# A new head: q and k further ahead, k's squares added on GpSimd, the column norms computed beside the last scores, and x and mean squares of two blocks interleaved

## The chip, the cores and the metric

The kernel runs on one core of one Trainium2 chip. The metric is device time in microseconds: the median of the timed runs of the whole program. One profiled execution of the kernel gives the trace that every row below comes from.

## What is computed

The reference is a channel attention followed by two feed-forward stages, all on 6016 tokens with 256 channels, in float32:

```python
qn = q / (norm(q, axis=1) + 1e-6)           # norm over the 6016 tokens, one per channel
kn = k / (norm(k, axis=1) + 1e-6)
s = kn.transpose(0, 2, 1) @ qn / tau        # 256 x 256
a = softmax(s)
x = v @ a                                   # 6016 x 256
xn = x / sqrt(mean(x*x, -1) + 1e-6) * rms_g
y = (silu(xn @ w_gate) * (xn @ w_val)) @ w_out      # inner width 1536
h = y @ w_in                                # inner width 2048
out = (h - tanh(h)) @ w_out2
```

## The kernel before

All large products after the head are made as three TensorE passes (`mm3`, L82 to L84): each operand is split into a high part (`hi_of`, ScalarE, L75) and a low part (`lo_of`, VectorE, L78). Weights arrive as pairs of 32-bit words and are converted by a generator, `conversion()`: for each block of 512 columns `wNraw` it runs a copy on ScalarE (L136, result `wNy`), a shift on VectorE (L183), two VectorE combinations (L189, L195), the split on ScalarE (L75, `wNh`) and the subtraction on VectorE (L78, `wNl`). One pump of the generator does one of four steps; `PLAN` says how many pumps run at each labelled place of the program, and `at(...)` runs them. A block that a product needs and that isn't converted yet is converted on the spot. Raw weights have three buffers, so a later weight load waits for a conversion; the order of loads is that of the program on SP's one queue. `("s", i)` labels the place after chunk `i` of the head, `("c", n)` places between the last scores and the first gate product, `("g", ...)` and `("h", ...)` places in the two feed-forward stages.

The order on each engine is that of the program text: the schedule is manual, and every engine works through its own list.

The head is `attention()`. q and k come in chunks of token rows; per chunk ScalarE squares q and k (L325; the first ones straight into `acc`, L321), VectorE adds them into `acc` (L326), and TensorE adds k-transposed times q into two accumulators `S0` and `S1` (L308, two products for each of the 47 rows of a chunk; the profile has two records for each float32 product, so 188 records, 16 for a chunk of 4 rows). The squares of the two are of one size and go through two `sq` buffers. The last two chunks' scores wait until `nrm` (L345), a product of `acc` with a column of ones, has given TensorE the sums of squares. VectorE then takes the inverse root (L354 to L362, 15 small operations), spreads q's factors over the partitions (`dq`, L366, then the product `rq_ps`, L370) and forms the softmax of the two halves (L381 to L392). The result `a` feeds `x` (L412), which is v times a for the first two blocks of 512 tokens.

The head is followed, block by block, by `x_post`: squares on ScalarE (L437), mean squares `ms` on TensorE (L479, eight narrow products per block), the inverse root on VectorE (L485 to L96), its spread over partitions (`d`, L491, product `r`, L497), `xg` (x times the gain, ScalarE L443, times `r`, VectorE L505), and the split of that into `x0h` and `x0l` for block 0, `x1h` and `x1l` for block 1. Blocks 0 and 1 are then multiplied by the gate and value weights, feature by feature: `g` and `v` (L82 to L84), silu on ScalarE (L545) and the product on VectorE (L546, `t`). Block 1's post-work is spread over the first features of block 0's products (`POST`).

Before the change the first four chunks are loaded ahead and chunk `i+4` after chunk `i`'s scores:

```python
r = sp.tile([P, W, C], F32, tag=f"raw{nm}", bufs=4, name=f"{nm}{i}")
...
load(i + 4)
if i in W_LOADS:
    j = W_LOADS.index(i)
    w_load(w_queue[j], *((sp, EARLY_RAW) if j < EARLY_RAW else ()))
```

Of the kernel before, what the change touches and what calls it, by code (L numbers as in the profile page):

```python
# [794 lines left out]
```

## Time and profile before

| what | value |
|---|---|
| median of 3 timed runs | 1209.13 us (1208.88 to 1210.33) |
| the profiled execution | 1206.14 us, of which 1204.3 us are its span |
| TensorE busy in the span | 1186.8 us (99%) |
| VectorE, ScalarE, GpSimd busy | 681.1, 536.2 and 0.7 us |
| mean granted TensorE clock | 0.995 |

The profiled execution lies 2.99 us below the median of the timed runs. A time below that is "in the span" counts from the first instruction of the execution. An idle time in a row is that of the row's engine just before the instruction, with the work that ended it. "PEclk" is the granted TensorE clock as a share of full speed, 1.00 for 2.4 GHz and 0.50 for 1.2 GHz.

### The profile page before, as it was taken

How to read it: one execution, taken by the hardware profiler on the slowest of the kernel's cores; microseconds unless marked ns; L12 is line 12 of the kernel's file. 1: busy time of each engine (PE TensorE's matmuls, PEld its weight loads, DVE VectorE, ACT ScalarE, POOL GpSimd, SP SyncE). 2: the span in 40 equal slices, each digit the busy share in tenths (PEclk: the TensorE clock that was granted, in tenths of full speed). 3: DMA queues.
4: the chain of work that ended last, by engine and by line, in shares of the span. 5: the costliest groups of instructions: out<-in, count | busy, mean ns of one | idle time of the engine just before them, and what ended most of it. 6: DMA issues, size and time to landing. Idle time of an engine off the chain costs nothing.

```text
span 1204.3 us, 13571 instructions
## 1 busy us (share of the span) xinstructions
PE 1186.8 (99%) x5310; PEld 988.9 (82%) x5310; DVE 681.1 (57%) x1119; ACT 536.2 (45%) x930; POOL 0.7 (0%) x6
## 2 busy tenths in 40 slices
PE   8889999999999999999999999999999999999998
PEld 6668888888888888888888888888888888888998
DVE  5888779653384384375356347347337437436534
ACT  6556556543343354254344344344335325425434
POOL 0000000000000000000000000000000000000000
PEclk9999999999999999999999999999999999999999
DMA  9534332001001000000000000100100000000000
GB/s 340 208 107 123 89 104 88 18 19 35 1 1 36 1 1 20 16 1 18 18 1 18 18 1 1 35 1 1 35 1 1 32 1 1 18 1 1 18 1 14
DMA packets 20640, 43.33 MB, mean 36 GB/s; under 512 B 1889, under 2 KB 3169, under 8 KB 20577
## 3 DMA queue, kind: packets, MB, share of 16 engines
q1 hardware_dynamic: 20576, 42.48, 10.5%
q8 instruction: 41, 0.67, 0.2%
q14 instruction: 23, 0.18, 0.0%
HBM read 36.31 MB, written 6.16 MB: 35 GB/s over the span
## 4 chain that ended last, share of the span: by engine, by line
PE 97%; DVE 1%; DMA 1%; ACT 0%; issue 0%; SPq 0%; DVEq 0%
PE h L84 7%; PE h L82 7%; PE out L82 7%; PE out L84 7%; PE out L83 7%; PE h L83 7%; PE g L82 5%; PE y L84 5%; PE y L82 5%; PE g L84 5%; PE y L83 5%; PE g L83 5%; PE v L82 5%; PE v L84 5%; PE v L83 5%; PE S L308 3%
## 5 line engine op out<-in xcount | busy, mean ns | idle before, releaser
L546 DVE TENSOR_TENSOR t<-t,v 128x512 f32<-128x512 f32 (+1 forms) x144 | 97.4, 676 | 227.9 <-PE v L84 219.4
L560 DVE TENSOR_TENSOR t<-h,t 128x512 f32<-128x512 f32 (+1 forms) x192 | 129.6, 675 | 48.9 <-ACT t L559 48.8
L545 ACT ACTIVATE t<-g 128x512 f32<-128x512 f32 (+1 forms) x144 | 84.6, 588 | 129.5 <-PE g L84 126.5
L559 ACT ACTIVATE t<-h 128x512 f32<-128x512 f32 (+1 forms) x192 | 110.5, 575 | 17.3 <-PE h L84 17.1
L308 PE MATMUL S<-q,k 128*128 128x256 f32 x188 | 43.9, 394 | 5.5 <-DMA k<-k_in 5.5
L308 PEld LDWEIGHTS S<-q,k 128*128 128x128 f32 x188 | 36.7, 198 | 11.9 <-DMA q<-q_in 4.3
L326 DVE TENSOR_TENSOR acc<-acc,sq 128x1024 f32<-128x1024 f32 (+2 forms) x24 | 26.4, 1113 | 14.7 <-ACT sq L325 14.3
L96 DVE SCALAR_TENSOR_TENSOR y<-sq,y 128x512 f32<-128x512 f32 (+1 forms) x27 | 18.0, 668 | 0.0
L93 DVE SCALAR_TENSOR_TENSOR sq<-y,sq 128x512 f32<-128x512 f32 (+1 forms) x27 | 18.0, 668 | 0.0
L95 DVE TENSOR_TENSOR sq<-sq,y 128x512 f32<-128x512 f32 (+1 forms) x27 | 18.0, 667 | 0.0
L325 ACT ACTIVATE sq<-q 128x1024 f32<-128x1024 f32 (+2 forms) x12 | 11.6, 967 | 11.3 <-DMA q<-q_in 9.3
L443 ACT ACTIVATE xg<-x,g_t 128x512 f32<-128x512 f32 (+1 forms) x24 | 15.9, 667 | 1.1 <-PE ms L479 1.1
L75 ACT ACTIVATE u_2h<-t 128x512 fp32r<-128x512 f32 (+1 forms) x12 | 7.5, 623 | 18.5 <-DVE t L546 18.5
L75 ACT ACTIVATE w_12h<-t 128x512 fp32r<-128x512 f32 (+1 forms) x12 | 7.5, 623 | 18.5 <-DVE t L560 14.4
L75 ACT ACTIVATE u_8h<-t 128x512 fp32r<-128x512 f32 (+1 forms) x12 | 7.5, 623 | 18.2 <-DVE t L546 18.2
L75 ACT ACTIVATE u_1h<-t 128x512 fp32r<-128x512 f32 (+1 forms) x12 | 7.5, 623 | 18.1 <-DVE t L546 18.1
L75 ACT ACTIVATE u_6h<-t 128x512 fp32r<-128x512 f32 (+1 forms) x12 | 7.5, 623 | 18.1 <-DVE t L546 18.1
L75 ACT ACTIVATE u_9h<-t 128x512 fp32r<-128x512 f32 (+1 forms) x12 | 7.5, 624 | 17.7 <-DVE t L546 17.7
L75 ACT ACTIVATE u_7h<-t 128x512 fp32r<-128x512 f32 (+1 forms) x12 | 7.5, 623 | 17.7 <-DVE t L546 17.7
L75 ACT ACTIVATE u_10h<-t 128x512 fp32r<-128x512 f32 (+1 forms) x12 | 7.5, 623 | 17.7 <-DVE t L546 17.7
L75 ACT ACTIVATE u_0h<-t 128x512 fp32r<-128x512 f32 (+1 forms) x12 | 7.5, 623 | 17.3 <-DVE t L546 17.3
L75 ACT ACTIVATE u_5h<-t 128x512 fp32r<-128x512 f32 (+1 forms) x12 | 7.5, 624 | 17.2 <-DVE t L546 17.2
(2051 smaller groups left out, 3602.7 us busy)
## 6 DMA issues: line engine op xcount, KB each, us to landing
vraw<-vT_in SPq DMA_DIRECT2D x11, 512.0 KB, 3.8
outT<-o SPq DMA_DIRECT2D x22, 256.0 KB, 2.0
q<-q_in SPq DMA_DIRECT2D x10, 512.0 KB, 7.1
k<-k_in SPq DMA_DIRECT2D x10, 512.0 KB, 7.9
q<-q_in SPq DMA_DIRECT2D x2, 256.0 KB, 3.6
k<-k_in SPq DMA_DIRECT2D x2, 256.0 KB, 3.9
wg0raw<-w_gate_in SPq DMA_DIRECT2D x1, 512.0 KB, 8.9
wv0raw<-w_val_in SPq DMA_DIRECT2D x1, 512.0 KB, 9.6
```

The source lines that it names most:

```text
L75: nc.scalar.activation(out=dst, in_=src, func=AF.Copy, scale=scale)
L82: nc.tensor.matmul(out, wh, xh, start=first, stop=False)
L83: nc.tensor.matmul(out, wl, xh, start=False, stop=False)
L84: nc.tensor.matmul(out, wh, xl, start=False, stop=last)
L93: lambda: nc.vector.scalar_tensor_tensor(out=t, in0=y, scalar=-0.5, in1=m, op0=ALU.mult, op1=ALU.mult),
L95: lambda: nc.vector.tensor_mul(out=t, in0=t, in1=y),
L308: nc.tensor.matmul(S[m][:, :C], kt[:, j, m * P:(m + 1) * P], qt[:, j, :], start=(i == 0 and j == 0), stop=(i == NCH - 1 and j == n - 1))
L326: nc.vector.tensor_add(out=acc[:, s, :n], in0=acc[:, s, :n], in1=sq[:, :n])
L545: nc.scalar.activation(out=t[:, :n], in_=g[:, :n], func=AF.Silu)
L546: nc.vector.tensor_mul(out=t[:, :n], in0=t[:, :n], in1=v[:, :n])
L559: nc.scalar.activation(out=t[:, :n], in_=o[:, :n], func=AF.Tanh)
L560: nc.vector.tensor_sub(out=t[:, :n], in0=o[:, :n], in1=t[:, :n])
```

## The change

The change rewrites the head and what follows it up to the first gate product.

- The chunks are 1, 1, 2, ten of 4, 2 and 1 rows, 15 as before (they were 1, 2, 1, nine of 4, 4, 2, 1). Eight chunks are loaded ahead of any score, not four, into six small buffers for the first chunks, four pairs as before, and the buffers of `bh` and `bl` for two later chunks. tau and the gain are loaded behind them.
- k's squares are added on GpSimd (`nc.gpsimd.tensor_add`), q's on VectorE as before. Both accumulators are folded from four to two to one row, each on its engine, so that `nrm` takes 4 products and not 8 (`add`, L320).
- Three chunks' scores wait behind `nrm` and not two: 7 rows, 7 products (14 records) for `S0` first, then 7 for `S1`. tau is put on q's norms. The spread of q's factors takes `r_` itself, broadcast as weights, times the identity, and the tiles `dq` and `d` are gone. It stands behind the first `S1` product.
- The softmax takes one fused multiply and maximum (`tensor_tensor_reduce`), k's factor as the scale of the exponential, and the division on VectorE; the table of silu is loaded behind it.
- In the x stage the products of two blocks are interleaved and `ms` stands behind the first five of eight; the squares of block 1 come behind r0.
- `PLAN` pumps 19 steps of the conversion from the head to the first gate product, where it pumped 28, and starts at chunk 9 and not at chunk 7.

```diff
 PLAN = {
-    ('s', 7): 1, ('s', 8): 1, ('s', 9): 1, ('s', 10): 1, ('s', 11): 1, ('c', 0): 2, ('c', 1): 3,
-    ('c', 2): 10, ('c', 3): 6, ('c', 4): 1, ('c', 5): 1, ('g', 0, 0): 2, ('g', 1, 0): 3,
...
+    ('s', 9): 2, ('s', 10): 2, ('s', 11): 2, ('s', 12): 2, ('s', 13): 1, ('c', 0): 2, ('c', 1): 1,
+    ('c', 2): 2, ('c', 3): 1, ('c', 4): 2, ('c', 5): 1, ('c', 6): 0, ('c', 7): 1, ('g', 0, 0): 2,
...
-    BEHIND = 2
-    W_LOADS = [1, 3, 5, 9, 11]
+    FIRST_CHUNKS, LAST_CHUNKS = [1, 1, 2], [2, 1]
+
+    BEHIND = 3
+    WARM = 5
...
+                    if i < NF:
+                        r = act.tile([P, W // 2, C], F32, tag="xs", bufs=6, name=f"{nm}{i}")
+                    elif i in LENT:
+                        r = act.tile([P, W, C], F32, tag=f"b{'hl'[s]}", name=f"{nm}{i}")
+                    else:
+                        r = sp.tile([P, W, C], F32, tag=f"raw{nm}", bufs=4, name=f"{nm}{i}")
...
+            def add(s, out, a, b):
+                (nc.vector, nc.gpsimd)[s].tensor_add(out=out, in0=a, in1=b)
+
+            AHEAD_LOADS = NF + 5
+            for i in range(AHEAD_LOADS):
                 load(i)
             nc.sync.dma_start(out=tau_t, in_=tau.to_broadcast([P, 1]))
             nc.sync.dma_start(out=g_t, in_=rms_g)
-
-            nrm = psum("nrm")
+            for _ in range(WARM):
+                nc.tensor.matmul(nrm[:, :P], ones, ones, start=True, stop=True)
+
+            early = {NF: [0], NF + 2: [1]}
...
                     nc.scalar.activation(out=sq[:, :n], in_=raw[i][s][:, :n], func=AF.Square)
-                    nc.vector.tensor_add(out=acc[:, s, :n], in0=acc[:, s, :n], in1=sq[:, :n])
...
+                    add(s, acc[:, s, :n], acc[:, s, :n], sq[:, :n])
+                for h in (2, 1):
+                    if t0 + n == NT - sum(x for x in LAST_CHUNKS if x <= h):
+                        for s in range(2):
+                            add(s, acc[:, s, :h], acc[:, s, :h], acc[:, s, h:2 * h])
                 if i < NCH - BEHIND:
...
-                load(i + 4)
...
+                if i >= NF:
+                    load(i - NF + AHEAD_LOADS)
+                for j in early.get(i, ()):
+                    w_load(w_queue[j], sp, EARLY_RAW)
+                if i - NF + AHEAD_LOADS == NCH - 1:
                     load_v(0)
+                    w_load(w_queue[2])
+                    w_load(w_queue[3])
                     load_v(1, "ah")
+                    w_load(w_queue[4])
                 at("s", i)
...
+            rest = [(i, j) for i in range(NCH - BEHIND, NCH) for j in range(chunks[i][1])]
+            for i, j in rest:
+                score(i, j, 0)
             at("c", 0)
...
+            for x, (i, j) in enumerate(rest):
+                if x == 1:
+                    for m in range(KC):
+                        nc.tensor.matmul(
+                            rq_ps[:, m * P:(m + 1) * P], r_[:, 2 * m:2 * m + 1].to_broadcast([P, P]),
+                            ident, start=True, stop=True)
+                score(i, j, 1)
...
+                nc.vector.tensor_tensor_reduce(
+                    out=s_, in0=S[m][:, :C], in1=rq, scale=1.0, scalar=-3.4028234e38, op0=ALU.mult,
+                    op1=ALU.max, accum_out=mx)
...
+                nc.vector.tensor_scalar_mul(out=a_full[m], in0=e_, scalar1=sm)
+
+            nc.scalar.activation(out=mx, in_=ones[:, :1], func=AF.Silu)
...
         at("c", 2)
-        xs = [[], []]
...
+        x_full((0, 0, 0), (0, 1, 0), (1, 0, 0), (0, 0, 1), (0, 1, 1))
         for c in range(KC):
-            xs[0].append(x_matmuls_full(0, c))
             p0["square"](c)()
-        xs[1].append(x_matmuls_full(1, 0))
+            p0["ms"](c)
+        at("c", 3)
+        x_full((1, 1, 0), (1, 0, 1), (1, 1, 1))
...
-        POST = [8, 4, 9]
+        POST = [6, 5, 9]
```

How the change moves instructions is shown at three places. The first is ScalarE's list at the end of the head, before: the squares `sq` of q (`_0`) and of k (`_1`) of the last four chunks, and the first copy of the third weight block, `w10y`, behind all of them.

```order
L325 ACTIVATE sq_1_303<-k_231 128x1024 [waits DMAHW4_49,DVE_49]
L325 ACTIVATE sq_0_321<-q_250 128x1024 [waits DMAHW5_49,DVE_49]
L325 ACTIVATE sq_1_324<-k_252 128x1024 [waits DMAHW6_49,DVE_49]
L325 ACTIVATE sq_0_336<-q_271 128x512 [waits DMAHW7_49,DVE_49]
L325 ACTIVATE sq_1_339<-k_273 128x512 [waits DMAHW0_49,DVE_49]
L325 ACTIVATE sq_0_342<-q_294 128x256 [waits DMAHW2_49,DVE_49]
L325 ACTIVATE sq_1_345<-k_296 128x256 [waits DMAHW3_49,DVE_49]
L136 ACTIVATE w10y<-w10raw 128x512
L75 ACTIVATE wv0h<-wv0y 128x512 [waits DVE_49]
```

The same place now: `w10y` stands ahead of the last six squares and waits for a DMA, and the split `wv0h` of the second weight block stands between the squares.

```order
L338 ACTIVATE sq_1_314<-k_220 128x1024 [waits DMAHW3_49,Pool_49]
L137 ACTIVATE w10y<-w10raw 128x512 [waits DMAHW3_49]
L338 ACTIVATE sq_0_329<-q_236 128x1024 [waits DMAHW4_49,DVE_49]
L338 ACTIVATE sq_1_332<-k_238 128x1024 [waits DMAHW5_49,Pool_49]
L76 ACTIVATE wv0h<-wv0y 128x512 [waits DVE_49]
L338 ACTIVATE sq_0_342<-q_254 128x512 [waits DMAHW6_49,Activation_49]
L338 ACTIVATE sq_1_345<-k_256 128x512 [waits DMAHW7_49,Pool_49]
L338 ACTIVATE sq_0_351<-q_272 128x256 [waits DMAHW0_49,DVE_49]
L338 ACTIVATE sq_1_354<-k_274 128x256 [waits DMAHW1_49,Pool_49]
```

So the last six squares moved behind a weight block's arrival. The second place is the list of SP, which issues the loads, around the load of that third weight block, before (k of chunk 9, then q and k of chunks 10 and 11):

```order
L300 DMA k_193<-k_in 128x1024 [waits DMAHW7_49,Activation_49]
L130 DMA w10raw<-w_out_in 128x2x512 [waits DMAHW0_49]
L300 DMA q_211<-q_in 128x1024 [waits DMAHW1_49,PE_49,Activation_49]
L300 DMA k_213<-k_in 128x1024 [waits DMAHW2_49,Activation_49]
L300 DMA q_229<-q_in 128x1024 [waits DMAHW3_49,PE_49,Activation_49]
```

And now, at the end of q and k (chunk 14):

```order
L310 DMA q_272<-q_in 128x256 [waits DMAHW0_49,PE_49,Activation_49]
L310 DMA k_274<-k_in 128x256 [waits DMAHW1_49,Activation_49]
L261 DMA vraw_276<-vT_in 128x2x512 [waits DMAHW2_49]
L131 DMA w10raw<-w_out_in 128x2x512 [waits DMAHW3_49]
L131 DMA wg1raw<-w_gate_in 128x2x512 [waits DMAHW4_49]
```

`w10raw` moved behind the last chunk and the first v block. The third place is VectorE's list ahead of block 1's first use of `r` (`xg_1`), in the first features of the gate stage, before:

```order
L78 TENSOR_TENSOR wv2l<-wv2y,wv2h 128x512 [waits Activation_49]
L93 SCALAR_TENSOR_TENSOR nart_594<-nary_593,narm_592 128x8
L95 TENSOR_TENSOR nart_594<-nart_594,nary_593 128x8 [waits DVE_49]
L96 SCALAR_TENSOR_TENSOR nary_593<-nart_594,nary_593 128x8 [waits DVE_49]
L491 TENSOR_SCALAR d_635<-ident,nary_593 128x128 [waits DVE_49]
L491 TENSOR_SCALAR d_635<-ident,nary_593 128x128 x3
L546 TENSOR_TENSOR t_2_654<-t_2_654,v_2_641 128x512 [waits PE_49,Activation_49]
L189 SCALAR_TENSOR_TENSOR w12y<-w12raw,w12y 128x512 [waits DMAHW2_49]
L78 TENSOR_TENSOR u_2l<-t_2_654,u_2h 128x512 [waits Activation_49]
L505 TENSOR_TENSOR xg_1_538<-xg_1_538,r_672 128x512 [waits PE_49]
```

And now:

```order
L197 SCALAR_TENSOR_TENSOR wg2y<-wg2raw,wg2y 128x512
L185 TENSOR_SCALAR wv2y<-wv2y 128x512 [waits Activation_49]
L79 TENSOR_TENSOR wg2l<-wg2y,wg2h 128x512 [waits Activation_49]
L191 SCALAR_TENSOR_TENSOR wv2y<-wv2raw,wv2y 128x512 [waits DMAHW1_49,DVE_49]
L197 SCALAR_TENSOR_TENSOR wv2y<-wv2raw,wv2y 128x512 [waits DVE_49]
L185 TENSOR_SCALAR w12y<-w12y 128x512 [waits Activation_49]
L79 TENSOR_TENSOR wv2l<-wv2y,wv2h 128x512 [waits Activation_49]
L565 TENSOR_TENSOR t_2_648<-t_2_648,v_2_616 128x512 [waits PE_49,Activation_49]
L191 SCALAR_TENSOR_TENSOR w12y<-w12raw,w12y 128x512 [waits DMAHW3_49,DVE_49]
L79 TENSOR_TENSOR u_2l<-t_2_648,u_2h 128x512 [waits Activation_49]
L524 TENSOR_TENSOR xg_1_510<-xg_1_510,r_666 128x512 [waits PE_49]
```

Here the conversion of `wg2`, `wv2` and the start of `w12` stands ahead of `xg_1`. From the second `x0l` to `xg_1`, that one counted, VectorE's list before has 12 operations of 512 columns, one shift, four `d`, two of 256 columns and 11 small ones; now it has 19 of 512 columns, four shifts, no `d`, two of 256 columns and 11 small ones.

## Rows read from the trace of the kernel before

**Rows 1.** Busy time of each engine by stretch (the stretch in us, its length, busy us and instructions of PE, PEld, DVE, ACT and POOL, the granted clock, the DMA share and GB/s).

```profile
0.00:10.00 10.00, 6.08 (x16) 4.26 (x16) 0.52 (x3) 4.49 (x8) 0.70 (x6) 1.00 0.74 215
10.00:20.00 10.00, 8.46 (x38) 7.21 (x39) 7.35 (x6) 5.94 (x6) 0.00 (x0) 1.00 0.97 388
20.00:30.00 10.00, 10.00 (x49) 8.79 (x48) 7.62 (x9) 8.10 (x9) 0.00 (x0) 1.00 1.03 416
30.00:40.00 10.00, 10.00 (x48) 8.81 (x47) 9.18 (x11) 7.35 (x9) 0.00 (x0) 1.00 0.99 370
40.00:50.00 10.00, 10.00 (x56) 9.02 (x55) 8.51 (x19) 4.65 (x8) 0.00 (x0) 1.00 0.62 212
...
90.00:95.00 5.00, 5.00 (x24) 4.14 (x23) 4.30 (x9) 2.84 (x5) 0.00 (x0) 1.00 0.18 18
```

**Rows 2.** Waits of PE in the first 130 us: line, what it waited for, us in total, times, longest.

```profile
PE S L308 <- DMA k<-k_in: 5.5, 4, 3.4
PE x L412 <- ACT a L392: 3.9, 1, 3.9
PE r L497 <- DVE d L491: 1.5, 1, 1.5
PE g L82 <- ACT x0h L75: 1.4, 1, 1.4
```

**Rows 3.** PE's timeline of the same stretch: start, length, operation, records, and the idle time ahead with what ended it.

```profile
10.95 3.69 PE L308 MATMUL S<-q,k 128*128 128x256 f32 x16 [1.20 <-DMA k<-k_in]
15.24 31.32 PE L308 MATMUL S<-q,k 128*128 128x256 f32 x144 [0.59 <-DMA k<-k_in]
46.39 1.84 PE L345 MATMUL nrm<-ones,acc 128*128 128x2 f32 x16
...
56.64 8.45 PE L412 MATMUL x<-vraw,a 128*128 128x512 f32 x12 [3.94 <-ACT a L392]
...
70.89 1.13 PE L497 MATMUL r<-d,ones 128*128 128x512 f32 x2
73.46 0.80 PE L82 MATMUL g<-x0h,wg0h 128*128 128x512 f32 x1 [1.44 <-ACT x0h L75]
...
76.21 0.50 PE L82 MATMUL v<-x0h,wv0h 128*128 128x512 f32 x1
...
86.14 1.13 PE L497 MATMUL r<-d,ones 128*128 128x512 f32 x2 [1.48 <-DVE d L491]
```

**Rows 4.** ScalarE's groups of instructions in the first 50 us: count, busy us, mean ns of one, idle time ahead.

```profile
L325 ACT ACTIVATE sq<-k 128x1024 f32<-128x1024 f32 x10 | 10.6, 1057 | 1.7 <-DMA k<-k_in 1.7
...
L136 ACT ACTIVATE w10y<-w10raw 128x512 f32<-128x512 f32 x1 | 0.7, 660 | 0.0
...
L325 ACT ACTIVATE sq<-k 128x512 f32<-128x512 f32 x1 | 0.6, 630 | 0.5 <-DVE acc L326 0.5
...
L325 ACT ACTIVATE sq<-k 128x256 f32<-128x256 f32 x1 | 0.4, 417 | 0.2 <-DVE acc L326 0.2
```

**Rows 5.** VectorE's groups in the first 56 us, with the same columns.

```profile
L326 DVE TENSOR_TENSOR acc<-acc,sq 128x1024 f32<-128x1024 f32 x20 | 24.3, 1224 | 14.5 <-ACT sq L325 14.3
L326 DVE TENSOR_TENSOR acc<-acc,sq 128x512 f32<-128x512 f32 x2 | 1.3, 690 | 0.1
...
L326 DVE TENSOR_TENSOR acc<-acc,sq 128x256 f32<-128x256 f32 x2 | 0.8, 422 | 0.1
```

**Rows 6.** GpSimd's timeline, all that runs longer than 0.1 us on it in the whole execution.

```profile
0.73 0.20 POOL masks.py:197 MEMSET ident<- 128x128 f32 x1 [0.29 <-POOLq L785]
1.01 0.29 POOL masks.py:199 TENSOR_SCALAR_AFFINE_SELECT ident<-ident 128x128 f32<-128x128 f32 x1
```

**Rows 7.** DMA issues of the first 60 us: count, KB each, median us from issue to landing.

```profile
vraw<-vT_in SPq DMA_DIRECT2D x2, 512.0 KB, 6.3
...
w10raw<-w_out_in SPq DMA_DIRECT2D x1, 512.0 KB, 8.2
wg1raw<-w_gate_in SPq DMA_DIRECT2D x1, 512.0 KB, 5.0
```

**Rows 8.** VectorE's timeline from 44 us on: the chain of the norms, the softmax and the post-work of the blocks.

```profile
48.27 0.17 DVE L354 TENSOR_SCALAR n__368<-nrm 128x8 f32<-128x8 f32 x1 [0.90 <-PE nrm L345]
...
51.16 0.20 DVE L362 RECIPROCAL r__385<-y__369 128x8 f32<-128x8 f32 x1
...
53.92 0.42 DVE L384 TENSOR_REDUCE mx<-s 128x1 f32<-128x256 f32 x1
...
73.59 1.48 DVE L78 TENSOR_TENSOR x0l<-xg,x0h 128x512 fp32r<-128x512 f32 x2
...
83.41 0.69 DVE L78 TENSOR_TENSOR u_1l<-t,u_1h 128x512 fp32r<-128x512 f32 x1
84.01 0.69 DVE L78 TENSOR_TENSOR wv2l<-wv2y,wv2h 128x512 fp32r<-128x512 f32 x1
...
88.00 0.68 DVE L505 TENSOR_TENSOR xg<-xg,r 128x512 f32<-128x512 f32 x1
```

**Rows 9.** The granted clock around two idle times of PE (stretch, length, PE's busy us and instructions, clock, DMA share, GB/s).

```profile
56.00:58.00 2.00, 1.36 (x2) 0.50 0.00 0
...
63.00:64.00 1.00, 1.00 (x3) 1.00 0.43 76
...
75.00:76.00 1.00, 1.00 (x4) 0.50 0.90 350
```

More of the change, by code (lines that the diff above doesn't have):

```diff
@@ L280, in attention @@
             W = 4
-            for n in [1, 2, 1] + [W] * ((NT - W - 1) // W - 1) + LAST_CHUNKS:
+            whole = (NT - sum(FIRST_CHUNKS) - sum(LAST_CHUNKS)) // W
+            for n in FIRST_CHUNKS + [W] * whole + LAST_CHUNKS:
                 chunks.append((t, n))
                 t += n
-            assert t == NT
-            H = W // 2
+            assert t == NT and sum(FIRST_CHUNKS) == W
+            NCH, NF = len(chunks), len(FIRST_CHUNKS)
+            LENT = [NF + 4, NF + 9]
             qr = q.rearrange("(p n) c -> p n c", p=P)
@@ L289, in attention @@
             S = [psum(f"S{m}") for m in range(KC)]
+            nrm = psum("nrm")
             raw = {}
-            NCH = len(chunks)
             def load(i):
@@ L343, in attention @@
                     c0 = 2 * (KC * s + m)
-                    for w in range(H):
-                        nc.tensor.matmul(
-                            nrm[:, c0:c0 + 2], acc[:, s, w, m * P:(m + 1) * P], ones[:, :2],
-                            start=w == 0, stop=w == H - 1)
-            for i in range(NCH - BEHIND, NCH):
-                scores(i)
+                    nc.tensor.matmul(
+                        nrm[:, c0:c0 + 2], acc[:, s, 0, m * P:(m + 1) * P], ones[:, :2],
+                        start=True, stop=True)
+            rest = [(i, j) for i in range(NCH - BEHIND, NCH) for j in range(chunks[i][1])]
+            for i, j in rest:
+                score(i, j, 0)
             at("c", 0)
@@ L359, in attention @@
             nc.vector.tensor_scalar_mul(
[L360 to L361 removed]
+                out=y_[:, :2 * KC], in0=y_[:, :2 * KC], scalar1=tau_t)
             nc.vector.reciprocal(out=r_, in_=y_)
[L364 to L367 removed]
@@ L486, in eps_narrow @@
             T["rs"] = rsqrt_ops(T["m"], T["yn"], T["t"])
[L488 to L493 removed]
         def spread():
             T["y"] = psum(f"r{b}")
[L497 removed]
+            for t in range(NG):
+                nc.tensor.matmul(
+                    T["y"][:, t * P:(t + 1) * P], T["yn"][:, 2 * t:2 * t + 1].to_broadcast([P, P]),
+                    ident, start=True, stop=True)
         def norm(c):
@@ L517, in x_post @@
                 square=square, gain=gain, ms=ms_narrow,
-                rs=[eps_narrow] + [rs(i) for i in range(10)] + [diag], spread=spread, norm=norm,
-                high=high, low=low)
+                rs=[eps_narrow] + [rs(i) for i in range(10)], spread=spread, norm=norm, high=high,
+                low=low)
         return ([square(c) for c in cs] + [sq_sum] + [gain(c) for c in cs]
@@ L682, in attn_moe_kernel @@
             p0["high"](c)()
-            at("c", 5 + c)
+            p1["gain"](c)()
+        for c in range(KC):
+            p1["ms"](c)
         for c in range(KC):
             p0["low"](c)()
+        at("c", 7)
         split_a()
```

118 lines of the change are left out of this document (43 added, 75 removed), and 5 rows, old and new, of the table PLAN.

## The prediction

> **What bounds the kernel now.** I read the waits of TensorE first, since it is busy for nearly the whole span and only its idle time, a low clock or less work on it can be won. In the head it waits 5.5 us for k, 3.9 us for the softmax, 1.5 us for block 1's spread and 1.4 us for block 0's first split [rows 2]. Its timeline shows where: the first 32 records of the scores wait for k, and from 15.24 us the next 144 run in 31.32 us without a gap, 0.2175 us each [rows 3]; `nrm` follows at 46.39, x at 56.64, the first gate product at 73.46 [rows 3]. The stretches show the loads at 388 to 416 GB/s from 10 to 30 us, and TensorE busy for 5.00 of 5.00 us from 90 us on [rows 1]. So whatever the change does before about 92 us reaches the end one for one, unless the new order makes a gap later.
>
> **The scores.** The first chunks and chunk 3 are 8 rows of q and k, 8 x 2 x 0.131 = 2.10 MB; the first 10 us of loading moved 10 x 215 = 2.15 MB [rows 1], so chunk 3's k is there at about 10.5. More chunks are out by then, so TensorE waits no more: it eats 1.05 MB in 16 x 0.2175 = 3.48 us, 301 GB/s, less than the loads bring [rows 1]. Chunks 3 to 11 are 144 records, 31.3 us [rows 3]: TensorE stands at `nrm` at 41.8, with 28 records left, where it came there at 46.39 with 12 left. With no wait the scores would end at 41.8 + 0.9 (`nrm`, half the records of the 1.84 us [rows 3]) + 6.1 = 48.8, about 2 us sooner than before. The products on ones ahead of the first chunk run while k is awaited and cost nothing.
>
> **The squares, the step that I think decides.** ScalarE now has `w10y` ahead of the last six squares, and `w10raw` is loaded behind all of q and k and the first v block. Two ways give its landing. By bytes: q and k 12.32 MB, and four blocks of 0.524, together 14.42 MB; before, 2.15 + 3.88 + 4.16 + 3.70 = 13.89 MB had moved at 40 us [rows 1], and the rest at 370 GB/s takes 1.4 us: 41.4. By issue: chunk 14 goes into chunk 9's buffer, free at 10.5 + 7 x 3.48 = 34.9; four issues later it is about 36.5, and 5.0 to 6.3 us to landing, as `wg1raw` and the v blocks took [rows 7], give 41.5 to 42.8. I take 42.5. The ends are 39.5 (all after the first 10 us at 416 GB/s) and 44.7 (the 8.2 us that `w10raw` took before [rows 7]). Queued behind the wait are 0.66 (`w10y`) + 1.06 + 1.06 (squares of chunk 12) + 0.63 (`wv0h`, like a square of its size) + 2 x 0.63 + 2 x 0.42 [rows 4] = 5.5 us: the last square is done at about 48.1, chunk 12's k square at 45.3.
>
> **GpSimd's adds.** No row shows a GpSimd add. Its only long rows are 0.20 us for a fill of 128 columns and 0.29 for an operation with one input [rows 6]. Lower bound: VectorE's own 1.22 us for 1024 columns [rows 5]. Upper: 0.29 - 0.1 for 128 columns, times 8, is 1.6 with its 0.1 us of start, and twice that for two inputs 3.1. I take 2.2, the middle, being nearer to neither. The Trainium skill, "GPSIMD Engine Reference", section 3.1, gives 4497 ns for such an add of 2048 columns and 2293 on VectorE; half of it, an estimate of 2.25 us, would change the sum by 0.1 us. After chunk 12's square GpSimd still has one add of 1024 columns, an add and a fold of 512, an add and a fold of 256, 2.5 times the large one: 5.5 us and some 0.5 us of handing over, so `nrm` can run at 45.3 + 6.0 = 51.3 (48.5 with the lower price, since the last square itself ends at 48.1; 53.5 with the upper). VectorE's half is done earlier: its adds cost 1.22, 0.69 and 0.42 us [rows 5].
>
> **From `nrm` to x.** TensorE idles from 41.8 to 51.3. Before, after an idle time of 3.94 us [rows 3] the clock stood at 0.50 from 56 to 58 us and was back at 1.00 from 63 [rows 9]; after 1.44 us it was 0.50 at 75 to 76 [rows 9], and g took six records in 76.21 - 73.46 = 2.75 us [rows 3]. So `nrm` and much of `S0`'s 14 records run at 0.50: 3.0 us at full speed, 6.1 at half; I take 4.7. `S0` ends at 51.3 + 0.9 + 4.7 = 56.9. The 15 small operations of the norm (48.27 to 51.36, 3.1 us [rows 8]) lie beside `S0` now, to 55.5, and that is the change's real gain. The first record pair of `S1` and the spread take 0.8 more. From the spread to x there were 3.94 us of idle time [rows 3]; the fused operation saves the maximum of 0.42 [rows 8] and the second half no longer stands between, some 1 us less: x at 56.9 + 0.8 + 2.9 = 60.6, 4.0 later than 56.64. The rest of `S1` is hidden in that time.
>
> **The x stage.** 16 records of 512 columns are 16 x 0.435 = 7.0 at full clock, `ms` of block 0 takes 1.7, its inverse root lies beside the last three x products, and from r to the first g it is 73.46 - 70.89 = 2.6 [rows 3], beside which block 1's `ms` runs. The first g comes at 60.6 + 11.3 = 71.9, 1.6 sooner than before, and without a drop of the clock, so v comes 2 to 3 us sooner. The x stage gives back 5.6 us: the slow clock of x, a second `ms` in the way, and the idle time ahead of g. The table of silu and the loads of tau and the gain are moved to where ScalarE and SP have time.
>
> **The conversions that were put off.** VectorE's list from the second `x0l` to `xg_1` had 12 operations of 512 columns, one shift, four `d`, two of 256 columns and 11 small ones: 12 x 0.60 (83.41 to 84.01) + 0.4 + 0.9 + 0.8 + 2.2 (0.20 apart) = 11.5 us of the 13.6 from 75.07 to 88.68 [rows 8]. Now it has 19, four, none, two and 11: at 0.60 to 0.72, as one of them waits for the other or not, I take 19 x 0.66 + 1.4 + 0.8 + 2.2 = 16.9, and 0.8 of waits, 17.7. `x0l` ends at 71.9 + 1.8 = 73.7, so `xg_1` ends at 91.4, 2.7 us after 88.68 [rows 8]. TensorE has only block 0's features to do until then, and waits. No wait and 0.60 each give +0.8; all the 2.2 us of waits and the dearer price +4.1.
>
> **The sum.** Scores ready sooner (-2.1), squares, adds and clock later (+6.1): x +4.0; the x stage -5.6; conversions ahead of `xg_1` +4.3: +2.7 us. The profiled execution of 1206.14 us becomes 1208.8. The median of the timed runs lies 2.99 above it: 1211.8, and I say 1212.
>
> **Rivals.** First, the adds themselves set `nrm`. GpSimd's chain for a chunk is square 1.06 + add + about 0.2, with one k buffer in turn, against TensorE's 3.48 us: from an add of 2.3 us on it falls behind by itself. If, besides, a VectorE add and a GpSimd add can't run together, a chunk takes 1.22 + 2.2 = 3.4 us of the two, ten chunks from 11.6 take until 45.8, and the folds, the last chunks and five conversions (5.5 + 4.1) come on top: `nrm` at 55 to 57, and 64 with 3.1 us an add. That is +7 to +16, by the middle price 1218. For it: VectorE is already busy for 9.18 of 10 us from 30 to 40 [rows 1], beside no GpSimd work at all, and the chains have no slack. Against it: q's half is taken off VectorE's load. The Trainium skill, "SBUF — State Buffer", section "Who interferes with whom", says that a VectorE instruction with two SBUF inputs and a GpSimd instruction that reads SBUF share a port that one of them holds for its whole length; by it this rival holds, and no row before can show it, GpSimd being idle. Chance 0.34.
>
> Second, the other side: `w10raw` is early. If it lands by 39.5 and an add takes 1.5 or less, `nrm` is ready at 46, 5.3 sooner than in my sum, and some of the clock is kept: -2 to -5 us, about 1206. It decides at an `nrm` of 48.5, where the sum is zero. For it: with eight chunks out from the start, the loads' slow first 10 us could be faster than 215 GB/s. Against it: chunk 14 can't be issued ahead of 34.9, whatever the rate. Chance 0.22.
>
> Third, that the deeper loads bring nothing: at 416 GB/s there is no more to have. If TensorE reaches `nrm` at 45 for that reason, it still waits until 51.3, and the time is the forecast's. It has no time of its own.
>
> **Chances and range.** The forecast has 0.44, with its own range from +0.8 to +5.5, 1210 to 1214.5; about 0.16 of it lies within 0.2% (2.4 us, about what a measurement here can tell from no change) and 0.28 above. The first rival adds 0.34 slower, the second 0.20 faster and 0.02 the same: 0.20, 0.18, 0.62. A range of 1205 to 1221 leaves out the dearer third of the first rival, 0.12, and the second's best, 0.06.
>
> **What would show it.** In the new profile: a wait of TensorE at `nrm` of 6 to 10 us, ended by an add on GpSimd, and a wait of ScalarE at `w10y` for the DMA, with `w10raw` landing at 41 to 44; a granted clock of 0.50 behind it; x at 59 to 62, the first g at 71 to 73; VectorE with no idle time from `x0l` to `xg_1` and TensorE waiting for that. GpSimd's add of 1024 columns shows my 2.2 right or wrong, VectorE's add beside it (1.22 or longer) the shared port. I am wrong if TensorE passes `nrm` without a wait, or if `xg_1` doesn't hold up block 1.

## The result, and the profile after

The changed kernel takes 1218.79 us (median of 4 runs, 1218.43 to 1219.14), beside 1209.01 of the kernel before: ratio 1.0082, interval 1.0065 to 1.0100, about 10 us slower. The profiled execution took 1219.14 us, 13.0 more than the profiled one of before: that one was 2.9 below its median, this one 0.35 above.

The waits of TensorE in the first 130 us, after (columns as in [rows 2]):

```profile
PE nrm L364 <- DVE acc L320: 15.4, 1, 15.4
PE S L315 <- DMA k<-k_in: 3.4, 3, 1.8
PE g L83 <- ACT x1h L76: 3.2, 2, 2.7
PE r L514 <- DVE nary L97: 1.9, 1, 1.9
```

The waits for the softmax and for `x0h` of [rows 2] are gone, as the change has it. One wait of 15.4 us took their place, at `nrm`, and one of 3.2 us at block 1's first products. TensorE's timeline says when:

```profile
11.71 31.32 PE L315 MATMUL S<-q,k 128*128 128x256 f32 x144 [1.81 <-DMA k<-k_in]
...
58.40 1.87 PE L364 MATMUL nrm<-ones,acc 128*128 128x2 f32 x8 [15.37 <-DVE acc L320]
60.13 5.36 PE L315 MATMUL S<-q,k 128*128 128x256 f32 x16
...
68.62 4.56 PE L434 MATMUL x<-vraw,a 128*128 128x512 f32 x10
...
80.08 0.48 PE L83 MATMUL g<-x0h,wg0h 128*128 128x512 f32 x1
...
100.35 0.50 PE L83 MATMUL g<-x1h,wg0h 128*128 128x512 f32 x1 [2.70 <-ACT x1h L76]
...
102.33 0.79 PE L83 MATMUL g<-x1h,wg0h 128*128 128x512 f32 x1 [0.47 <-ACT x1h L76]
...
108.44 0.39 PE L83 MATMUL g<-x0h,wg2h 128*128 128x512 f32 x1
```

Before, the last two of these places, block 1's first product and block 0's next (with `wg2h`), stood at:

```profile
91.21 0.39 PE L82 MATMUL g<-x1h,wg0h 128*128 128x512 f32 x1
...
95.29 0.39 PE L82 MATMUL g<-x0h,wg2h 128*128 128x512 f32 x1
```

TensorE runs its scores without a gap from 11.71 us, where it did from 15.24 [rows 3], but with 16 records behind it and not 32. At the 160th of all 188 records both kernels stand alike: 11.71 + 31.32 = 43.03 now, 15.24 + 128 x 0.2175 = 43.08 before. So the deeper loads brought nothing there; TensorE comes to `nrm` sooner only because 28 records wait behind it and not 12.

`nrm` ran at 46.39 [rows 3]; now it runs at 58.40. x comes 12.0 us later than its 56.64, the first gate product only 6.6 later than 73.46 [rows 3], so the x stage gives back 5.4. Block 1's first product stood at 91.21 and stands at 100.35, 9.1 later. The last 4.0 us come between it and block 0's next product (95.29 to 108.44 is 13.1), with the wait for the second half of `x1h` and a lower clock, seen in TensorE's stretches (stretch, length, busy us and instructions, granted clock, DMA share, GB/s):

```profile
50.00:55.00 5.00, 0.00 (x0) 0.50 0.00 0
55.00:60.00 5.00, 1.60 (x8) 0.50 0.01 2
60.00:65.00 5.00, 5.00 (x17) 0.65 0.44 107
65.00:70.00 5.00, 4.90 (x22) 1.00 0.01 3
98.00:100.00 2.00, 0.00 (x0) 1.00 0.41 159
100.00:101.00 1.00, 0.65 (x2) 1.00 0.00 0
101.00:103.00 2.00, 1.53 (x4) 0.51 0.04 8
103.00:106.00 3.00, 3.00 (x9) 0.50 0.19 12
106.00:108.00 2.00, 2.00 (x7) 0.53 0.65 244
108.00:110.00 2.00, 2.00 (x10) 1.00 0.20 17
```

Why `nrm` is late is read from GpSimd and VectorE side by side. GpSimd's timeline:

```profile
30.37 2.36 POOL L320 TENSOR_TENSOR acc<-acc,sq 128x1024 f32<-128x1024 f32 x1 [1.17 <-ACT sq L338]
33.89 2.38 POOL L320 TENSOR_TENSOR acc<-acc,sq 128x1024 f32<-128x1024 f32 x1 [1.17 <-ACT sq L338]
37.44 3.18 POOL L320 TENSOR_TENSOR acc<-acc,sq 128x1024 f32<-128x1024 f32 x1 [1.17 <-ACT sq L338]
```

VectorE's timeline in the same stretch:

```profile
31.40 2.40 DVE L320 TENSOR_TENSOR acc<-acc,sq 128x1024 f32<-128x1024 f32 x1 [1.13 <-ACT sq L338]
34.41 2.14 DVE L185 TENSOR_SCALAR wg0y<-wg0y 128x512 int32<-128x512 int32 x1 [0.60 <-ACT wg0y L137]
36.58 0.69 DVE L191 SCALAR_TENSOR_TENSOR wg0y<-wg0raw,wg0y 128x512 int32<-128x512 int32 x1
37.19 1.22 DVE L320 TENSOR_TENSOR acc<-acc,sq 128x1024 f32<-128x1024 f32 x1
38.33 2.84 DVE L197 SCALAR_TENSOR_TENSOR wg0y<-wg0raw,wg0y 128x512 int32<-128x512 int32 x1
41.09 0.41 DVE L185 TENSOR_SCALAR wv0y<-wv0y 128x512 int32<-128x512 int32 x1
```

The same add takes 1.22 us when GpSimd is idle at its start and 2.40 when it starts within a GpSimd add: the add at 31.40 ends at 33.80, 1.07 us after GpSimd's at 32.73. GpSimd's own add, 2.35 us when VectorE has nothing running at its start, takes 3.18 when it starts 0.25 us after VectorE's. Each waits for the other's whole instruction, and the profile writes that wait into the busy time. So too the conversions: 2.14 for a shift that takes 0.41 with GpSimd idle (41.09), 2.84 for a combination of 0.69. That is what the Trainium skill, "SBUF — State Buffer", section "Who interferes with whom", states, and by which the first rival held.

ScalarE, third, hands the delay on to the squares, in its own order:

```profile
36.30 1.06 ACT L338 ACTIVATE sq<-k 128x1024 f32<-128x1024 f32 x1 [0.42 <-POOL acc L320]
41.20 0.63 ACT L76 ACTIVATE wg0h<-wg0y 128x512 fp32r<-128x512 f32 x1 [3.84 <-DVE wg0y L197]
...
43.63 0.65 ACT L137 ACTIVATE w10y<-w10raw 128x512 f32<-128x512 f32 x1
...
52.98 0.63 ACT L76 ACTIVATE wv0h<-wv0y 128x512 fp32r<-128x512 f32 x1 [5.65 <-DVE wv0y L197]
```

`w10y`, on which my forecast rested, starts at 43.63 without any wait: `w10raw` was issued at 37.5 and landed 5.5 us later, at 43.0. Two splits of weights wait 3.84 and 5.65 us for VectorE, which is held by GpSimd, and the squares of chunks 11 to 14 are queued behind these splits.

### The profile page after: what moved, and what is told of

It reads as the page before. It is cut to its first block, busy times and chain, and to the rows that moved or that the text cites. A ratio compares the mean times of both kernels' runs of the same rounds, so it can differ in the third digit from the quotient of the medians.

```text
span 1217.4 us, 13604 instructions
## 1 busy us (share of the span) xinstructions
PE 1189.1 (98%) x5332; PEld 992.6 (82%) x5332; DVE 683.5 (56%) x1096; ACT 535.9 (44%) x929; POOL 30.9 (3%) x20
## 4 chain that ended last, share of the span: by engine, by line
PE 94%; DVE 3%; DMA 1%; ACT 1%; issue 1%; SPq 0%; ACTq 0%; DVEq 0%
PE h L85 7%; PE h L83 7%; PE out L85 7%; PE out L83 7%; PE out L84 7%; PE h L84 7%; PE y L85 5%; PE y L83 5%; PE y L84 5%; PE v L84 5%; PE v L85 5%; PE v L83 5%; PE g L83 5%; PE g L84 5%; PE g L85 5%; PE S L315 2%
## 5 line engine op out<-in xcount | busy, mean ns | idle before, releaser
L320 DVE TENSOR_TENSOR acc<-acc,sq 128x1024 f32<-128x1024 f32 (+2 forms) x12 | 20.7, 1723 | 19.2 <-ACT sq L338 19.2
L320 POOL TENSOR_TENSOR acc<-acc,sq 128x1024 f32<-128x1024 f32 (+2 forms) x12 | 27.8, 2315 | 26.4 <-ACT sq L338 26.4
L364 PE MATMUL nrm<-ones,acc 128*128 128x2 f32 x8 | 1.9, 355 | 15.4 <-DVE acc L320 15.4
L338 ACT ACTIVATE sq<-k 128x1024 f32<-128x1024 f32 (+2 forms) x12 | 11.6, 966 | 10.5 <-POOL acc L320 10.3
L76 ACT ACTIVATE u_7h<-t 128x512 fp32r<-128x512 f32 (+1 forms) x12 | 7.5, 623 | 17.7 <-DVE t L565 17.7
L76 ACT ACTIVATE u_9h<-t 128x512 fp32r<-128x512 f32 (+1 forms) x12 | 7.5, 624 | 17.7 <-DVE t L565 17.7
L76 ACT ACTIVATE u_10h<-t 128x512 fp32r<-128x512 f32 (+1 forms) x12 | 7.5, 623 | 17.7 <-DVE t L565 17.7
```

Source lines behind the costliest of these rows:

```text
L76: nc.scalar.activation(out=dst, in_=src, func=AF.Copy, scale=scale)
L320: (nc.vector, nc.gpsimd)[s].tensor_add(out=out, in0=a, in1=b)
```

## The experiments

The question: is `nrm` late because VectorE and GpSimd exclude each other (sharing), because of the order on ScalarE (my forecast's step, "late block"), or because a GpSimd add is slow by itself? Ratios are to the kernel before on the same chip, with their intervals; times of `nrm` and x are from the profiles.

| run | `nrm` at | x at | median us | ratio |
|---|---|---|---|---|
| changed kernel | 58.4 | 68.6 | 1218.79 | 1.0082 [1.0065, 1.0100] |
| e1: k's adds on VectorE | 51.9 | 62.4 | 1214.32 | 1.0060 [1.0043, 1.0076] |
| e2: e1, w10raw earlier | 51.5 | 62.7 | 1212.56 | 1.0043 [1.0028, 1.0058] |
| e3: no conversion in the head | 49.7 | 60.6 | 1221.38 | 1.0116 [1.0096, 1.0136] |
| e4: q's squares in PSUM | 53.4 | 63.7 | 1214.90 | 1.0062 [1.0047, 1.0077] |
| e5: e1, plan spread out | 45.5 | 56.6 | 1202.75 | 0.9960 [0.9947, 0.9972] |
| e6: before, new x stage | 46.4 | 56.6 | 1205.72 | 0.9981 [0.9972, 0.9991] |
| e7: changed, block 1's post-work early | 57.9 | 68.4 | 1214.61 | 1.0060 [1.0045, 1.0075] |
| e8: e5 and e7 together | 45.6 | 55.6 | 1204.26 | 0.9973 [0.9963, 0.9982] |
| e9: e5, k's adds on GpSimd | 52.7 | 63.6 | 1210.49 | 1.0018 [1.0008, 1.0027] |
| e10: e9, q's squares in PSUM | 45.8, 48.7 | 58.8 | 1204.86 | 0.9975 [0.9966, 0.9984] |
| e11: e5, five chunks ahead | 45.3 | 55.4 | 1203.01 | 0.9965 [0.9953, 0.9976] |
| e12: e1, weights behind the squares | 46.9 | 57.7 | 1208.09 | 1.0005 [0.9995, 1.0015] |

**e1, one part undone.**

```diff
-                (nc.vector, nc.gpsimd)[s].tensor_add(out=out, in0=a, in1=b)
+                nc.vector.tensor_add(out=out, in0=a, in1=b)
```

> Only edit: k's adds back on VectorE, everything else as changed. Sharing theory (a VectorE operation with two SBUF inputs and a GpSimd add exclude each other): VectorE's adds fall from 2.40 to 1.22 us, its conversions in the head from 1.7-2.8 to 0.69, nrm comes at 46 to 49 instead of 58.4, x at 55 to 58, and the time is 1205 to 1210 us. Late-block theory (my forecast's: w10y waits for w10raw ahead of the last squares): w10raw still lands at 43, nrm stays at 50 or later, ScalarE shows a wait for the DMA at w10y of several us, and the time is 1211 to 1214.

VectorE's adds were at 1.2 us each and its conversions at 0.69, as the sharing theory says, but `nrm` came at 51.9, where the late-block theory put it, and the time was a little above that theory's. In its profile `nrm` comes 6.5 us sooner and x 6.2. By the ratios the time falls by 2.7 us, and their intervals overlap; the two profiled executions, 1219.14 and 1213.83 us, lie 5.3 apart. With the sharing gone ScalarE shows what it had covered:

```profile
41.92 0.66 ACT L137 ACTIVATE w10y<-w10raw 128x512 f32<-128x512 f32 x1 [2.72 <-DMA w10raw<-w_out_in]
...
47.76 0.63 ACT L76 ACTIVATE wv0h<-wv0y 128x512 fp32r<-128x512 f32 x1 [3.29 <-DVE wv0y L197]
```

**e2, the third weight block loaded earlier.** With e1's edit:

```diff
-            early = {NF: [0], NF + 2: [1]}
+            early = {NF: [0], NF + 2: [1], NF + 4: [2]}
...
-                    w_load(w_queue[j], sp, EARLY_RAW)
+                    w_load(w_queue[j], *((sp, EARLY_RAW) if j < EARLY_RAW else ()))
...
-                    w_load(w_queue[2])
```

> As the run before, and the third weight block (w10raw) is loaded behind chunk 7's squares and not behind all of q and k. Late-block theory: nrm 3 us sooner than in the run before, and 2 to 3 us less time. Sharing theory: GpSimd is idle, the block's place matters only as far as ScalarE waits for it: 0 to 1 us.

`w10y` no longer waited, and `nrm` came only 0.4 us sooner: the split behind it took the wait over, and VectorE with it. That is the sharing theory's 0 to 1 us and not the 3 of the late block. The median fell by 1.8 us, which the intervals don't separate, and the trace doesn't show a gain: block 1's first product comes at 94.67, in e1 at 94.12.

```profile
40.54 0.66 ACT L137 ACTIVATE w10y<-w10raw 128x512 f32<-128x512 f32 x1
...
47.39 0.63 ACT L76 ACTIVATE wv0h<-wv0y 128x512 fp32r<-128x512 f32 x1 [4.22 <-DVE wv0y L197]
```

**e3, the adds alone on both engines.** The nine steps of the conversion between the chunks are moved to place c2, behind the softmax.

```diff
-    ('s', 9): 2, ('s', 10): 2, ('s', 11): 2, ('s', 12): 2, ('s', 13): 1, ('c', 0): 2, ('c', 1): 1,
-    ('c', 2): 2, ('c', 3): 1, ...
+    ('c', 0): 2, ('c', 1): 1,
+    ('c', 2): 11, ('c', 3): 1, ...
```

> The changed kernel, with the nine conversion steps between the chunks moved behind the softmax (place c2); the adds stay as they are. Sharing theory: with only its own adds VectorE keeps the pace of 3.5 us a chunk to the end as it did up to 36 us, and nrm comes at 51 to 52 instead of 58.4; x at about 61; what is won there is lost again by nine more steps ahead of block 1's xg: 1215 to 1222. If GpSimd's adds alone set nrm it stays at 56 to 58. Late-block theory: w10y no longer stands in the squares, nrm at 51.

As the sharing theory has it. GpSimd works at one chunk in 3.52 us up to the last large one, VectorE's 2.40 fit into the rest of the chunk, and TensorE's pace of 3.48 is nearly kept; `nrm` runs at 49.7 for q and 51.1 for k. GpSimd's, VectorE's and ScalarE's timelines in e3:

```profile
36.43 2.35 POOL L320 TENSOR_TENSOR acc<-acc,sq 128x1024 f32<-128x1024 f32 x1 [1.17 <-ACT sq L338]
39.95 2.35 POOL L320 TENSOR_TENSOR acc<-acc,sq 128x1024 f32<-128x1024 f32 x1 [1.17 <-ACT sq L338]
```

```profile
37.46 2.40 DVE L320 TENSOR_TENSOR acc<-acc,sq 128x1024 f32<-128x1024 f32 x1 [1.13 <-ACT sq L338]
40.99 2.39 DVE L320 TENSOR_TENSOR acc<-acc,sq 128x1024 f32<-128x1024 f32 x1 [1.12 <-ACT sq L338]
```

```profile
38.81 1.06 ACT L338 ACTIVATE sq<-k 128x1024 f32<-128x1024 f32 x1 [1.38 <-POOL acc L320]
```

So the adds on two engines set `nrm` at about 51 without any conversion between them: k's square waits 1.38 us for the `sq` buffer that GpSimd's add still reads, and square and add together make the 3.52. With all adds on VectorE and a better order `nrm` comes at 45.5 to 46.9 (e5, e12), so a GpSimd add of 2.35 us has a price of its own. The nine conversions bring `nrm` 7 us further back, by collision and by their place on ScalarE. What was won came back behind x, where TensorE waited 5.4 us for a square on ScalarE that stood behind the moved steps.

**e4, the collision taken from q's adds alone.** q's squares go to PSUM, in pieces of 512, so that VectorE's add reads one input there.

```diff
+                    if s == 0:
+                        for h in range(0, n, 2):
+                            e = min(h + 2, n)
+                            sq = ps_a.tile([P, W // 2, C], F32, tag="a", name=f"sq{i}_0_{h}")
+                            nc.scalar.activation(
+                                out=sq[:, :e - h], in_=raw[i][s][:, h:e], func=AF.Square)
+                            add(s, acc[:, s, h:e], acc[:, s, h:e], sq[:, :e - h])
+                        continue
```

> The changed kernel, with q's squares written to PSUM in pieces of 512, so that VectorE's adds have one input in SBUF; k's adds stay on GpSimd. If two SBUF inputs are what collides: VectorE's adds take 0.69 us for 512 columns beside a running GpSimd add, GpSimd's stay at 2.35, only the conversions still stretch; nrm at 53 to 57, time 1213 to 1218. If any VectorE operation on SBUF collides: the adds stretch to 2 us and more, and the time is 1218 to 1222. Late-block theory: no change, 1218 to 1220.

It came out as for two SBUF inputs. GpSimd's timeline in e4, then VectorE's:

```profile
12.20 2.36 POOL L320 TENSOR_TENSOR acc<-acc,sq 128x1024 f32<-128x1024 f32 x1 [10.90 <-ACT sq L346]
...
35.88 2.50 POOL L320 TENSOR_TENSOR acc<-acc,sq 128x1024 f32<-128x1024 f32 x1 [3.02 <-ACT sq L346]
```

```profile
13.00 1.28 DVE L320 TENSOR_TENSOR acc<-acc,sq 128x512 f32<-128x512 f32 x2 [1.31 <-ACT sq L341]
...
36.08 2.59 DVE L185 TENSOR_SCALAR wv0y<-wv0y 128x512 int32<-128x512 int32 x1
```

Two adds from PSUM, from 13.00 to 14.28, take 1.28 us together while GpSimd is in the middle of its add (12.20 to 14.56); the shift, with one input and that in SBUF, still waits for GpSimd and takes 2.59. Both engines still write the tile `acc`, so a wait for the tile is not what stretched the adds. The edit also leaves both `sq` buffers to k, so that its squares no longer wait for GpSimd's add of the chunk before; the 5.0 us that `nrm` gains hold both effects.

**e5, the order repaired.** With e1: weight blocks loaded behind chunks 3, 4 and 6, one step of the conversion a chunk, and four steps in VectorE's wait for the spread.

```diff
-    ('s', 9): 2, ('s', 10): 2, ('s', 11): 2, ('s', 12): 2, ('s', 13): 1, ('c', 0): 2, ('c', 1): 1,
-    ('c', 2): 2, ('c', 3): 1, ('c', 4): 2, ('c', 5): 1, ('c', 6): 0, ('c', 7): 1, ...
+    ('s', 8): 1, ('s', 9): 1, ('s', 10): 1, ('s', 11): 1, ('s', 12): 1, ('c', 0): 2, ('c', 8): 4, ('c', 1): 1,
+    ('c', 2): 5, ('c', 3): 2, ('c', 4): 2, ('c', 5): 2, ('c', 6): 0, ('c', 7): 2, ...
...
-            early = {NF: [0], NF + 2: [1]}
+            early = {NF: [0], NF + 1: [1], NF + 3: [2]}
...
             nc.vector.reciprocal(out=r_, in_=y_)
+            at("c", 8)
```

> k's adds on VectorE; the first three weight blocks loaded earlier (behind chunks 3, 4 and 6); the conversion at one step a chunk from chunk 8 to 12, four steps in the wait for q's spread, and 16 steps from there to the first gate product: 25 in all, where the changed kernel has 19. Theory now: beside the sharing, ScalarE's splits and copies of weights wait for VectorE or a load and hold the squares queued behind them. Then nrm comes at 44 to 47 (51.5 with the changed plan and k on VectorE), TensorE idles under 5 us there, and the time is 1 to 5 us below the kernel before. Rival: VectorE's 20 adds of 1.22 us themselves set nrm, at 49 or later; then the time stays within 3 us of the kernel before, or above.

As expected, and the fastest of the study: 4.7 us below the kernel before. TensorE waits 2.3 us at `nrm`, and 0.8 us is left of the wait for x1h. TensorE's timeline in e5:

```profile
45.45 1.46 PE L364 MATMUL nrm<-ones,acc 128*128 128x2 f32 x8 [2.32 <-DVE acc L321]
...
56.56 4.56 PE L435 MATMUL x<-vraw,a 128*128 128x512 f32 x10
...
69.55 0.54 PE L84 MATMUL g<-x0h,wg0h 128*128 128x512 f32 x1
...
86.92 0.50 PE L84 MATMUL g<-x1h,wg0h 128*128 128x512 f32 x1
```

**e6, the new x stage alone.** The kernel before, its head and its `PLAN` kept, with the x stage, `x_post` and `x_matmul_full` of the change:

```diff
-        xs = [[], []]
+        xs = [[psum(f"x{b}_{c}") for c in range(KC)] for b in range(2)]
...
+        x_full((0, 0, 0), (0, 1, 0), (1, 0, 0), (0, 0, 1), (0, 1, 1))
         for c in range(KC):
             p0["square"](c)()
+            p0["ms"](c)
```

> The kernel before with the new x stage alone (interleaved blocks, mean squares behind five of eight products, spread from broadcast weights); its head and its plan of 28 steps stay. If the x stage alone is worth what I said (a second mean square out of the way, no diagonal), the first gate product comes 2 to 3 us sooner than 73.5 and the time falls by 1 to 3 us. If what the x stage gives back is only the clock that the changed head kept, it is 0, and with the ten and six steps of the conversion inside the stage it may lose 1 to 2 us.

Not settled. The first gate product came at 73.44, no sooner than 73.46 [rows 3], and block 1's first product at 91.39 (91.21 before), which is the second expectation; yet the medians differ by 1.7 us with an interval that leaves out 1. The profiled execution was 1206.34 us, 0.2 more than the 1206.14 of before, so the traces can't show where 1.7 us went. The ten executions on record say a part of it: the five with a mean granted clock of 0.995 to 0.997 took 1203.9 to 1205.2 us, the five at 0.994, the profiled one among them, 1206.2 to 1206.7. Of the 21 executions of before on that chip none was above 0.994.

**e7, block 1's post-work early; e8, with e5.**

```diff
-        POST = [6, 5, 9]
+        POST = [11, 9, 9]
```

> The changed kernel with block 1's post-work run earlier: all of its inverse root behind feature 0, spread and norms behind feature 1, so that the forced conversion of wg2 and wv2 stands behind xg_1 and not ahead of it. If the conversions ahead of xg_1 hold TensorE: its waits for x1h (3.2 us) go, the clock isn't lowered there, and the time falls by 3 to 5 us against the changed kernel (ratio to before 1.004 to 1.006 instead of 1.008). If TensorE then waits for wg2 or wv2 instead: 0 to 1 us.

> The plan of the first run of this group and the earlier post-work of block 1 together. If both hold up something of their own, the gains add: 4 to 8 us below the kernel before.

In e7 the wait for x1h is gone, and TensorE waits 3.4 us for `r` where it waited 1.9, with the clock at 0.50 from 91 to 93 us behind that. Block 0's product with `wg2h` comes at 104.47 where it came at 108.44, and the profiled execution takes 4.0 us less, within the 3 to 5 expected; by the ratios, 1.0082 and 1.0060 with overlapping intervals, it is 2.7. So that the wait goes is shown, its price only roughly. In e8 nothing is added to e5 (0.9973, intervals overlap): the wait for `r` is 2.2 us, and that for x1h was 0.8 to begin with. The gains don't add.

**e9 and e10, GpSimd in the repaired order.** e9 is e5 with the one line of e1 as the change has it; e10 adds the edit of e4.

> The kernel of the spread plan (k's adds on VectorE, nrm at 45.5, 4.7 us below the kernel before) with one edit: k's adds on GpSimd again. Sharing theory: the adds go back to one chunk in 3.5 us, every conversion that starts beside a GpSimd add takes up to 2.8 us, nrm comes at 51 to 55, and the time is 3 to 9 us above that of the spread plan: 1206 to 1212, ratio to before 0.999 to 1.004. If the sharing only looked costly because of where the conversions stood: nrm at 48 or sooner, and within 1.5 us of the spread plan.

> The run before, with q's squares in PSUM, so that only the conversions and folds collide with GpSimd's adds, and k's squares have two buffers of their own. Sharing theory: a good part comes back, nrm at 46 to 50, and the time is within 3 us of the spread plan, ratio 0.995 to 0.999. If a GpSimd add of 2.35 us is itself too slow for the head: nrm at 50 or later, as in the run before.

Both came out within the sharing theory's bounds. From VectorE to GpSimd the one edit costs 0.0058 of the time, 7.0 us, and moves `nrm` from 45.5 to 52.7, 7.2 us. VectorE's timeline in e9:

```profile
31.98 1.21 DVE L321 TENSOR_TENSOR acc<-acc,sq 128x1024 f32<-128x1024 f32 x1
33.12 2.86 DVE L192 SCALAR_TENSOR_TENSOR wg0y<-wg0raw,wg0y 128x512 int32<-128x512 int32 x1
...
40.94 2.58 DVE L186 TENSOR_SCALAR wv0y<-wv0y 128x512 int32<-128x512 int32 x1
```

With q in PSUM most of it comes back (0.9975), again with both `sq` buffers for k. What is left is GpSimd's tail: TensorE waits 2.26 us between q's half of `nrm` at 45.8 and k's at 48.7. So of the 7.2 us at `nrm` 4.0 go with the collisions and the buffers, and 3.2 stay with GpSimd's longer chain of adds.

**e11, fewer loads ahead; e12, the squares freed in e1's order.**

```diff
-            AHEAD_LOADS = NF + 5
+            AHEAD_LOADS = NF + 2
```

> The spread plan's kernel with five chunks of q and k loaded ahead of any score and not eight, everything else the same. If the deeper loads bring what I credited them with (scores at pace from about 10.7 us and not 15.2), TensorE comes to nrm 2 to 4 us later and the time rises by 1 to 4 us. If VectorE's adds set nrm anyway (45.5): the time stays within 1.5 us.

No difference (0.9965 and 0.9960): `nrm`, at 45.3 and 45.5, waits for VectorE in both, so the sixth to eighth chunk needn't be ahead. TensorE ran its scores without a gap from 11.7 us all the same and stood at the 160th record at 43.0, as before the change with four chunks ahead.

```diff
-    ... ('s', 11): 2, ('s', 12): 2, ('s', 13): 1, ...
+    ... ('s', 11): 1, ('s', 14): 4, ...
```

> k's adds on VectorE and the changed plan (nrm at 51.9, 7.0 us above the kernel before), with one more edit: the last four conversion steps ahead of nrm stand behind all squares, so that w10y and wv0h no longer lie between them on ScalarE. If those two hold the squares, as my forecast had it: nrm at 47 to 48.5, x 3 to 4 us sooner, and the time 2 to 4 us lower, ratio to before 1.0025 to 1.0045. If VectorE's own load sets nrm: nrm at 51 or later and no change.

The step of my forecast, together with the second wait that it left out: with `w10y` and `wv0h` behind the squares `nrm` comes 5.0 us sooner than in e1 (46.9), and the ratio falls from 1.0060 to 1.0005, 6.6 us, more than the 2 to 4 expected. x starts 4.7 us sooner (57.7 for 62.4).

## Why the prediction was right, and where it wasn't

The direction and the range held; of the cases, the first rival came true (1218, measured 1218.8) and not the likeliest (1212). The step that failed is "the squares, the step that I think decides". `w10raw` landed at 43.0 as worked out (42.5), but nobody waited for it: ScalarE was 3.84 us late by then, by a split that waited for VectorE, and the next one waited 5.65. The sum took VectorE's operations at the durations of [rows 5] beside a working GpSimd, and put the chance of the contrary at 0.34. The Trainium skill's rule in "SBUF — State Buffer", "Who interferes with whom", names VectorE instructions with two SBUF inputs, as the adds and the combinations are.

That the time fell into the range is in part luck. The forecast went from the profiled execution to the median by adding 2.99 us; after the change the median lies 0.35 below the profiled one. The 13.0 us that the profile shows would have made 1222.1 by that step, above 1221. The closeness of the rival's 1218 is of the same kind.

In the forecast's own terms, in the profile: x +12.0 (forecast +4.0), the x stage -5.4 (-5.6), the conversions +4.2 (+4.3), then -1.9 and +4.0 that it did not have: +12.9 of the 13.0, where it had +2.7. Of its signs, TensorE's wait at `nrm` was there, but 15.4 us for 6 to 10, and the last add before it was VectorE's (done at 58.35, GpSimd's at 58.06); ScalarE's wait at `w10y` for the load was not there.

Point by point:

- TensorE at pace: 10.5 forecast, 11.7; at `nrm` 41.8 forecast, 43.0. The 1.2 us that the sum took from the deeper loads were not there (43.03 and 43.08 at the same record). On that the third rival was right, and it cost nothing, since TensorE waits at `nrm` anyway.
- A GpSimd add: 2.2 forecast, 2.35 measured when nothing holds it up; the upper bound of 3.1 is reached only when it waits (3.18, 3.32). The estimate of 2.25 us from the Trainium skill, "GPSIMD Engine Reference", section 3.1, came a little nearer.
- `nrm`: 51.3 forecast, 55 to 57 by the rival, 58.4 measured. The rival's sum left out that ScalarE's splits hold the squares while VectorE is held. Without the sharing (e1) `nrm` came at 51.9. So the forecast's number was, by luck, that of a kernel without GpSimd, and that by way of two waits, for `w10raw` and for `wv0y`, of which it had only the first (e2); freeing both gave 46.9 (e12).
- `nrm` to x: 9.3 forecast, 10.2 measured, the clock at 0.50 for most of the `S0` records.
- x to the first gate product: 11.3 forecast, 11.5 measured; the x stage gave back 5.4 us where 5.6 were forecast. The stage's order alone moves nothing in the trace (e6). What does, the clock (1.00 at x now, 0.50 before [rows 9]) or the fewer conversion steps inside the stage, no run separates.
- second `x0l` to `xg_1`: 17.7 forecast, 81.80 to 99.63 = 17.8 measured (ends of VectorE's two rows below: 81.11 + 0.69 and 98.95 + 0.68), against 13.6 [rows 8]. But before, TensorE had 1.9 us of other work behind x1h (88.71 + 0.63 to 91.21), which my sum didn't count as cover. After its wait at 100 it waited once more and the clock fell, which it didn't price: 100.35 to 108.44 is 8.1 us, before 4.1 (91.21 to 95.29), so 4.0 against nothing forecast. Of these, ten products from 103.35 to 107.62 follow each other at 0.427 us, all at the lower clock; before it was 0.227, which makes 2.0.
- Two bounds of the sums are off, without moving the forecast: an `nrm` by the lower price of an add is 45.3 + 2.5 x 1.22 + 0.5 = 48.9 and not 48.5, and all the waits with the dearer price make +5.3 ahead of `xg_1` and not +4.1.

```profile
81.11 0.69 DVE L79 TENSOR_TENSOR x0l<-xg,x0h 128x512 fp32r<-128x512 f32 x1 [0.41 <-ACT x0h L76]
...
98.95 0.68 DVE L524 TENSOR_TENSOR xg<-xg,r 128x512 f32<-128x512 f32 x1
```

And the row of ScalarE before the change from which the 1.9 us count:

```profile
88.71 0.63 ACT L75 ACTIVATE x1h<-xg 128x512 fp32r<-128x512 f32 x1 [0.80 <-DVE xg L505]
```

How the loss divides depends on the order of undoing. Alone, taking the adds off GpSimd gives 2.7 us by ratios that don't separate, 5.3 by the profiled executions (e1), since the order of ScalarE then sets `nrm`; in the repaired order the same edit is worth 7.0 (e9 against e5). Shown are the sharing, by the durations (changed kernel, e4, e9), the held squares (e12) and the wait behind the conversions ahead of block 1 (e7). Not separated are the price of the sharing and that of GpSimd's slower adds and of the `sq` buffers. Only argued is the low clock's part in the last 4 us, since no run changed it alone.
